# Value products of the one-lane steps on 40 stationary columns in two column halves of the array

## The chip, the core and the metric

The kernel runs on one core of a Trainium2 chip. The metric is device time in microseconds (us) of one execution. PE is TensorE's stream of matmuls and PEld its weight loads, DVE is VectorE, ACT is ScalarE, POOL is GpSimd, and SP is SyncE, whose queue issues nearly all of the DMAs.

## The reference: what is computed

A sequence of 2048 tokens of width 640 passes through two pairs of layers, A B A B, each with a residual and a layer norm ahead of it. A is attention with a recurrent memory: the tokens are cut into 64 segments of 32, and the 8 rows of memory that segment s reads are rows of the output of segment s - 1. So the segments of A are sequential. B is a token mixer and MLP (640 to 640 to 640, 640 to 1536 to 640).

```
for s in range(n_seg):
    h = jnp.concatenate([mem, xs], axis=1)          # 8 + 32 = 40 rows
    q = jnp.einsum('btd,dhe->bhte', h, Wq)          # 32 heads of 192; k and v alike
    scores = jnp.einsum('bhqe,bhke->bhqk', q, k) * scale
    scores = jnp.where(mask[None, None], scores, -1000000000.0)
    p = _softmax(scores, axis=-1)
    o = jnp.einsum('bhqk,bhke->bhqe', p, v)
    o = jnp.einsum('bhte,hed->btd', o, Wo)
    mem = o[:, :M, :].copy()
    outs.append(o[:, M:, :])
```

All is bfloat16 with sums in fp32. The weights of both A layers are the same, and so are those of both B layers.

## The kernel before

**Lanes and steps.** The first A layer is lane 0 and the second is lane 1, five segments behind (LAG, line 22). There are 69 steps. Step t works on segment t of lane 0 and segment t - 5 of lane 1, side by side in one 80-column tile hT (lane 0 in columns 0 to 39, lane 1 in 40 to 79). In steps 0 to 4 only lane 0 has a segment, in steps 64 to 68 only lane 1. These ten are the one-lane steps. In them a product whose moving operand is hT moves 56 columns in place of 80 (ONE, W at line 538).

**Inside a step.** The 32 heads are 8 groups of 4 heads (GW = 768 columns of a weight matrix), taken as 4 pairs of groups. proj_pair (line 549) makes k, q and v of a pair, attend (line 658) does scores, softmax, the product with v and the output product Wo of one group. B is done in chunks of 64 tokens of both lanes, one chunk every two steps, mixed into the steps' work; a last chunk stands alone behind step 68.

**Values.** In a two-lane step v is made transposed, as k and q are: 30 matmuls for each group (line 578), a copy, six transposes (line 616) and two copies into V. In a one-lane step `values` (lines 631 to 658) is called for every pair (V_ONE, line 28). It makes v with tokens as rows: hT is the stationary operand, all 80 columns of it, and the weights move, 384 columns at a time. For each group j of a pair and each half hf of its 768 columns, five matmuls (kc = 0 to 4) add up in one PSUM tile of 80 by 384, so a pair has 20 matmuls in four tiles, each in a bank of its own. Four copies bring them to V: half 0 on ACT (line 656), half 1 on DVE (line 654). The rows of the lane without a segment are computed and copied too. V, like qT, kT, Pm and PT, has one buffer, so V of a group can be written only when the product of the group before has read it.

**Weights.** Of the weight matrices a part stays in SBUF after its first load and the rest is streamed in every step: of the five slices (kc) of a pair, two or three of k, q and v each come through a ring of nine tiles "wst" of 384 KB (RING_A, line 25; issue at line 476), which also wait on SP for a slot to come free. The order of pairs turns round from step to step, so the first pair of a step uses what the last pair of the step before left in the ring (KEEP). B's weights come through a ring of three "wstB" tiles (lines 512 to 518). Wo stays in SBUF after step 0.

**Order.** No loop sets the order of instructions. Each operation is given to a planner (`add`, lines 99 to 138) with its engine, a cost in us, a due time, and what it reads and writes. `place` (from line 140) runs a list schedule with these costs, with PSUM banks and ring slots as resources (class A has six banks, class B two), and the program is written in the order that comes out. An engine runs its instructions in that order. A matmul of n moving columns is put down as max(54, n) / 2400 + 0.0025 us (mm_us), so a group of five value matmuls costs 0.8125 us in the plan.

Of the kernel before, what the change touches and what calls it, by code (L numbers as in the profile page):

```python
# [9 lines left out]
ACT = mybir.ActivationFunctionType  # L10
ALU = mybir.AluOpType
AX = mybir.AxisListType
bf16 = mybir.dt.bfloat16
f32 = mybir.dt.float32
# [7 lines left out]
HG = 4  # L22
# [3 lines left out]
RING_B = 3  # L26
STEP = 48.0
V_ONE = (0, 1, 2, 3)
V_ON = ("ACT", "DVE")
V_PARTS = (range(0, 5),)  # L30
KEEP = True
WO_FROM = 1
AT = (0.0, 0.2, 0.5)
# [9 lines left out]
VT_BUFS = 1  # L43
# [49 lines left out]
class Plan:  # L93
# [8 lines left out]
    def add(self, e, d, due, fn, r=(), w=(), a=(), dma=0, queue=None, margin=0.0, after=()):  # L102
        op = Op()
        op.e, op.d, op.due, op.fn, op.dma, op.margin = e, d, due, fn, dma, margin
        op.succ, op.ready, op.n = [], 0.0, 0
        op.i = len(self.ops)
        op.paced = False
        op.last = None
        op.after = after
        preds = set(after)  # L110
        slots = []
        for b in r:
            preds.update(b.writers)
        for b in w:
            preds.update(b.writers)
            preds.update(b.readers)
        for b in a:
            preds.update(b.base)
            preds.update(b.readers)
        for b in r:  # L120
            b.readers.append(op)
        for b in w:
            b.base = [op]
            b.writers = [op]
            b.readers = []
        for b in a:
            b.writers.append(op)
        for b in {id(b): b for b in (*r, *w, *a)}.values():
            if isinstance(b, Slotted):
                b.left += 1  # L130
                slots.append(b)
        op.slots = slots
        preds.discard(op)
        for p in preds:
            p.succ.append(op)
            op.n += 1
        self.ops.append(op)
        if queue is not None:
            self.queues.setdefault(queue, []).append(op)
        return op  # L140
# [122 lines left out]
def kernel(  # L263
# [16 lines left out]
    nc = tc.nc  # L280
    P = 128
    _, S, Dm = A_x.shape
    H, Dh = A_Wq.shape[1], A_Wq.shape[2]
    M = A_mem0.shape[1]
    SEG = int(A_seg_len)
    NSEG = S // SEG
    F = B_w3.shape[1]
    KC = Dm // P
    FC = F // P
    assert (Dm, F, Dh, H, SEG, M) == (640, 1536, 192, 32, 32, 8) and S % (2 * SEG) == 0 and NSEG > 8  # L290
    NG = H // HG
    GW = HG * Dh
    GC = GW // P
    GWH = GW // 2
    PW = 2 * GW
    NPAIR = NG // 2
    L1 = SEG + M
    NS = 2 * L1
    QD = Dm // 4
    VP = 2 * Dh + 64  # L300
    scale = float(Dh) ** -0.5
# [26 lines left out]
    def ctile(shape, dtype, name):  # L328
        return const.tile(shape, dtype, name=name)
# [35 lines left out]
    Vt = [ctile([NS, 2 * VP], bf16, f"V{i}") for i in range(VT_BUFS)]  # L365
# [3 lines left out]
    Pm = Pmw[:].rearrange("p (c n) -> p c n", c=HG)  # L369
# [42 lines left out]
    def B(*key):  # L412
        key = ALIAS.get(key, key)
        if key not in bufs:
            bufs[key] = Buf()
        return bufs[key]
# [5 lines left out]
    add = plan.add  # L422

    def ps(cls, shape, dtype, name):
        b = Slotted(cls, None)

        def make():
            return psum.tile(shape, dtype, name=name, tag=f"{cls}{b.slot}")
        b.make = make
        return b  # L430

    def T(b):
        if b.obj is None:
            b.obj = b.make()
        return b.obj

    def mm_us(n, m=128, k=1):
        return k * (max(54, n) / 2400.0 + 0.0025)

    def dve_us(n, ps_=True):  # L440
        return ((120 if ps_ else 58) + n) / 960.0 + 0.02

    def act_us(n, ps_=True):
        return ((172 if ps_ else 224) + n) / 1200.0 + 0.02
# [89 lines left out]
    def HX(t):  # L534
        return [B("hT", t % 4, k) for k in ("x0", "m", "xa", "xb", "xc")]

    def attention_step(t):
        ln = lanes(t)
        both = len(ln) == 2
        c0 = 0 if 0 in ln else L1  # L540
        N = NS if both else L1
        NR = c0 + N
# [4 lines left out]
        base = t * STEP  # L547
        sl = STEP / NG
        h = hT[t % 4]
        hk = HX(t)  # L550
# [4 lines left out]
        def proj_pair(i_, pr):  # L555
            s0 = base + sl * 2 * i_
            for kind, at in zip("kqv", AT):
# [9 lines left out]
                for j in range(2):  # L567
# [36 lines left out]
                    else:  # L604
                        V_ = Vt[G % VT_BUFS]

# [12 lines left out]
                        for hf in range(2):  # L619
                            def fe(op, pvt=pvt, V_=V_, hf=hf):  # L620
                                src = T(pvt)[0:NS, GWH * hf:GWH * (hf + 1)].rearrange("n (a b) -> n a b", a=2)
                                v0 = hf * (VP - 64)
                                dst = V_[:, v0:v0 + 512].rearrange("n (a b) -> n a b", a=2)[:, :, 64 * hf:64 * hf + Dh]
                                if hf:
# [5 lines left out]

        def values(i_, pr, s0, wbs, wv):
            nres = KC - STREAM["v"] + MORE.get(("v", pr), 0)
            pv = [[ps("A", [NS, GWH], f32, "psv") for _ in range(2)] for _ in range(2)]
            for j in range(2):
                for hf in range(2):
                    for kcs in V_PARTS:
                        def fv(op, j=j, hf=hf, kcs=kcs):
                            a = GW * j + GWH * hf
                            for kc in kcs:
                                nc.tensor.matmul(out=T(pv[j][hf])[:], lhsT=h[:, kc, :], rhs=wv(kc, a, a + GWH),  # L640
                                                 start=(kc == 0), stop=(kc == KC - 1))
                        rb = [wbs[0]] if kcs[0] < nres else []
                        rb += [wbs[1 + kc - nres] for kc in kcs if kc >= nres]
                        add("PE", mm_us(GWH, k=len(kcs)), s0 + (0.2 * j + 0.05 * hf) * sl, fv,
                            r=(*rb, *hk), a=(pv[j][hf],))
            for j in range(2):
                V_ = Vt[(t * NG + 2 * i_ + j) % VT_BUFS]
                for hf in range(2):
                    def fe(op, j=j, hf=hf, V_=V_):
                        v0 = hf * (VP - 64)  # L650
                        dst = V_[:, v0:v0 + 512].rearrange("n (a b) -> n a b", a=2)[:, :, 64 * hf:64 * hf + Dh]
                        src = T(pv[j][hf])[:].rearrange("n (a b) -> n a b", a=2)
                        if V_ON[hf] == "DVE":
                            nc.vector.tensor_copy(out=dst, in_=src)
                        else:
                            nc.scalar.copy(out=dst, in_=src)
                    add(V_ON[hf], dve_us(GWH) if V_ON[hf] == "DVE" else act_us(GWH), s0 + 0.2 * sl * j, fe, r=(pv[j][hf],),
                        w=(B("V", (t * NG + 2 * i_ + j) % VT_BUFS, hf),))

        def attend(p_, g):  # L660
            G = t * NG + p_
            s0 = base + sl * p_
            q, k_, V_ = qT, kT[G % KT_BUFS], Vt[G % VT_BUFS]
            pss = ps("A", [P, HG * NS], f32, "pss")
            hi = s0 + HI[2] * sl

            def fs(op):
# [8 lines left out]
                r=(B("qT"), B("kT", G % KT_BUFS, 0), B("kT", G % KT_BUFS, 1), B("kT", G % KT_BUFS, 2)), w=(pss,))  # L676
            sm_ = sm[G % 2]
            Pb = Pm
# [8 lines left out]

            def f2(op):
                o = T(pss)[0:NR, 0:HG * N].rearrange("p (a b) -> p a b", a=HG)
                nc.scalar.activation(out=Pb[0:NR, :, c0:c0 + N], in_=o, func=ACT.Exp, bias=sm_[0:NR, 0:1], scale=-1.0)  # L690
            add("ACT", act_us(HG * N) + 0.09, hi - HI[0], f2, r=(pss, smk), w=(Pk,))

            def f3(op):
                nc.vector.tensor_reduce(out=sm_[0:NR, 2:2 + HG], in_=Pb[0:NR, :, c0:c0 + N], axis=AX.X, op=ALU.add)
                nc.vector.reciprocal(out=sm_[0:NR, 6:6 + HG], in_=sm_[0:NR, 2:2 + HG])
                nc.vector.tensor_tensor(out=Pb[0:NR, :, c0:c0 + N], in0=Pb[0:NR, :, c0:c0 + N],
                                        in1=sm_[0:NR, 6:6 + HG].unsqueeze(2).to_broadcast([NR, HG, N]), op=ALU.mult)
            add("DVE", 0.53 + 0.0085 * N, hi - HI[0], f3, w=(Pk, B("sm4", G % 2)))
            pst = ps("A", [P, HG, NS], bf16, "pst")
# [39 lines left out]
            for hf in range(2):  # L739
                def f8(op, hf=hf):  # L740
                    o = T(psy)
                    for cc in range(3 * hf, 3 * hf + 3):
                        for m in range(KC):
                            st = first_wo[0]
                            first_wo[0] = False
                            nc.tensor.matmul(out=o[:, m, cw:cw + W], lhsT=wo[:, cc, m * P:(m + 1) * P],  # L746
                                             rhs=o_[:, cc, 0:W], start=st, stop=True, skip_group_check=True)
                add("PE", mm_us(W, k=3 * KC), due, f8, r=(wb, oks[hf]), a=(psy,))

        for i_ in range(NPAIR):  # L750
            pr = NPAIR - 1 - i_ if t % 2 and KEEP else i_
# [562 lines left out]
    for o in placed:  # L1314
        k = len(nc.cur_bb.bb.instructions)
# [6 lines left out]
        elif o.paced:  # L1322
            k = len(done) - 1
# [39 lines left out]
```

## Time and profile before

| | |
|---|---|
| median of 9 runs | 3435.96 us (3427.66 to 3443.72) |
| the profiled execution | 3437.28 us, span 3435.6 us |
| PE busy | 3329.0 us, 97% of the span |
| PEld busy | 3207.8 us, 93% |
| DVE, ACT, POOL busy | 2394.3 us, 1678.1 us, 236.6 us |
| read from HBM | 817.14 MB, 239 GB/s over the span |
| granted TensorE clock, mean | 0.993 |

Busy time of PE counts a matmul's record from its start to its end, and records of neighbouring matmuls overlap, so its share says little about how much room there is. What a matmul costs in a stream is the distance from its start to the start of the next, called its slot here. A step's borders are taken from the copy at line 765, which runs once near the end of each step and of which the profile has 68, from 89.0 to 3365.2 us.

### The profile page before, as it was taken

The page shows a single profiled execution, that of the slowest core. Times are in us where ns is not written, and L with a number is a line of the kernel's source. Part 1 is how long each engine was busy: PE and PEld are TensorE (multiplying, and loading weights), DVE is VectorE, ACT ScalarE, POOL GpSimd, SP SyncE. Part 2 cuts the span into 40 slices and gives each one's busy share as a digit, 9 for nine tenths or more (in the row PEclk, how much of TensorE's full clock was granted, in tenths as well). Part 3 has the DMA queues.
Part 4 walks back from the last instruction along what each step waited for, and adds up shares of the span by engine and source line. Part 5 has one row for each costly group of instructions (what it writes and reads, how often), then busy time and mean ns, then how long its engine had stood idle before and what let it go on. Part 6 is the DMA issues. An engine that isn't in the chain of part 4 may idle for free.

```text
span 3435.6 us, 183284 instructions
## 1 busy us (share of the span) xinstructions
PE 3329.0 (97%) x82491; PEld 3207.8 (93%) x82493; DVE 2394.3 (70%) x7359; ACT 1678.1 (49%) x4045; POOL 236.6 (7%) x488
## 2 busy tenths in 40 slices
PE   6999999999999999999999999999999999999998
PEld 4889999999999999999999999999999999999886
DVE  2667777777777677777767777776777777767665
ACT  1335555555554555455545555554555555455333
POOL 1000000000000000000000000000000000000000
PEclk8999999999999999999999999999999999999999
DMA  9777667766776686677667766776776677667775
GB/s 373 242 272 261 229 228 250 256 221 223 257 246 224 225 275 233 206 243 256 229 219 265 239 219 232 261 238 220 242 255 224 221 257 247 225 222 273 258 258 188
DMA packets 409739, 834.28 MB, mean 243 GB/s; under 512 B 39632, under 2 KB 207263, under 8 KB 408952
## 3 DMA queue, kind: packets, MB, share of 16 engines
q1 hardware_dynamic: 401656, 809.47, 68.9%
q8 instruction: 645, 10.57, 1.2%
q0 software_dynamic: 7136, 13.00, 1.2%
q14 instruction: 142, 1.16, 0.1%
q10 hardware_dynamic: 160, 0.08, 0.0%
HBM read 817.14 MB, written 5.24 MB: 239 GB/s over the span
## 4 chain that ended last, share of the span: by engine, by line
PE 93%; DMA 3%; issue 2%; ACT 1%; DVE 1%; SPq 1%; POOL 0%; POOLq 0%; ACTq 0%
PE psy L746 16%; PE psq L578 16%; PE psk L578 16%; PE psv L578 15%; PE pvt L616 5%; PE pso L719 4%; PE pss L672 4%; PE psv L640 3%; PE psh L1157 3%; PE y L1202 3%; PE pst L705 2%; PE psh L1035 1%; DMA wst<-in_A_Wv_dram 1%; PE hs L1094 1%; PE psv L808 1%
## 5 line engine op out<-in xcount | busy, mean ns | idle before, releaser
L578 PEld LDWEIGHTS <-wst 128*128 128x128 bf16 x24468 | 993.5, 99 | 23.9 <-issue 11.9
L746 PE MATMUL psy<-oT,wo 128*128 128x80 bf16 (+1 forms) x16560 | 660.2, 200 | 12.2 <-DMA wo<-in_A_Wo_dram 6.8
L746 PEld LDWEIGHTS <-wo 128*128 128x128 bf16 x16560 | 613.3, 99 | 15.1 <-DMA wo<-in_A_Wo_dram 7.6
L588 ACT CAST qT<-psq 128x480 bf16<-128x480 f32 (+1 forms) x552 | 291.7, 528 | 319.5 <-PE psq L578 310.0
L731 DVE CAST oT<-pso 128x240 bf16<-128x240 f32 (+1 forms) x552 | 214.3, 388 | 329.7 <-ACT oT L729 321.4
L578 PE MATMUL psk<-hT,wst 128*128 128x80 bf16 (+1 forms) x9108 | 428.7, 200 | 2.6 <-issue 1.9
L578 PE MATMUL psq<-hT,wst 128*128 128x80 bf16 (+1 forms) x8280 | 399.5, 199 | 4.4 <-issue 2.4
L578 PE MATMUL psq<-hT,wq 128*128 128x80 bf16 (+1 forms) x8280 | 376.9, 200 | 10.7 <-DVE V L625 5.7
L729 ACT CAST oT<-pso 128x240 bf16<-128x240 f32 (+1 forms) x552 | 189.7, 344 | 393.4 <-PE pso L719 369.8
L690 ACT ACTIVATE Pm<-pss,sm 80x320 bf16<-80x320 f32 (+2 forms) x552 | 279.4, 506 | 195.9 <-DVE sm L683 195.1
L578 PE MATMUL psk<-hT,wk 128*128 128x80 bf16 (+1 forms) x7452 | 348.6, 200 | 15.2 <-ACT hT L765 10.8
L578 PE MATMUL psv<-hT,wst 128*128 128x80 bf16 x7080 | 348.3, 202 | 7.4 <-issue 6.1
L602 DVE CAST kT<-psk 64x160 bf16<-64x160 f32 (+1 forms) x1104 | 336.3, 305 | 14.7
L578 PEld LDWEIGHTS <-wq 128*128 128x128 bf16 x8280 | 326.7, 99 | 16.9 <-issue 11.1
L578 PE MATMUL psv<-hT,wv 128*128 128x80 bf16 x7080 | 333.3, 202 | 3.6 <-issue 3.5
L578 PEld LDWEIGHTS <-wk 128*128 128x128 bf16 x7452 | 299.8, 99 | 24.6 <-issue 22.5
L710 ACT COPY PT<-pst 80x320 bf16<-80x320 bf16 (+1 forms) x552 | 222.3, 403 | 202.5 <-PE pst L705 198.5
L683 DVE CUSTOM_DVE_ANT_1 pss<-pss,mask 80x320 f32<-80x320 f32 (+2 forms) x552 | 252.2, 476 | 97.8 <-PE pss L672 94.9
L627 ACT COPY V<-pvt 80x384 bf16<-80x384 bf16 x472 | 223.8, 474 | 191.4 <-PE pvt L616 172.6
L578 PEld LDWEIGHTS <-wv 128*128 128x128 bf16 x7080 | 291.4, 100 | 8.7 <-issue 4.1
L608 ACT CAST vF<-psv 128x480 bf16<-128x480 f32 x472 | 261.8, 555 | 77.1 <-PE psv L578 71.9
L596 DVE CAST kT<-psk 128x320 bf16<-128x320 f32 (+1 forms) x552 | 254.6, 461 | 60.0 <-PE psk L578 53.2
(145 smaller groups left out, 4787.3 us busy)
## 6 DMA issues: line engine op xcount, KB each, us to landing
wst<-in_A_Wk_dram SPq DMA_DIRECT2D x555, 384.0 KB, 5.1
wst<-in_A_Wq_dram SPq DMA_DIRECT2D x486, 384.0 KB, 5.2
wst<-in_A_Wv_dram SPq DMA_DIRECT2D x486, 384.0 KB, 5.3
wstB<-in_B_w_dram SPq DMA_DIRECT2D x495, 320.0 KB, 4.7
wstB<-in_B_w_dram SPq DMA_DIRECT2D x132, 160.0 KB, 4.5
wo<-in_A_Wo_dram SPq DMA_DIRECT2D x8, 960.0 KB, 12.6
xw<-in_A_x_dram POOLq DMA_DIRECT2D x31, 80.0 KB, 5.2
x2d<-vbg POOLq DMA_DIRECT2D x31, 80.0 KB, 5.1
```

What stands on the lines that cost most here:

```text
L578: nc.tensor.matmul(out=o[:, cc, 0:W], lhsT=wv(kc, GW * j + cc * P, GW * j + (cc + 1) * P), rhs=h[:, kc, cw:cw + W], start=(kc == 0 and cc ...
L588: nc.scalar.copy(out=q[:, :, c0:c0 + N], in_=T(pq)[:, :, off:off + N])
L596: nc.vector.tensor_copy(out=k4[:, :, 0::3, c0:c0 + N], in_=p4[:, :, 0::2, off:off + N])
L602: nc.vector.tensor_copy(out=k4[r0:r1, :, jj, c0:c0 + N], in_=p4[r0:r1, :, 1, off:off + N])
L608: nc.scalar.copy(out=vF[:, :, c0:c0 + N], in_=T(pq)[:, :, off:off + N])
L627: nc.scalar.copy(out=dst, in_=src)
L683: nc.vector.tensor_tensor_reduce(out=o, in0=o, in1=maskt.unsqueeze(1).to_broadcast([NR, HG, N]), scale=-scale, scalar=3.0e38, op0=ALU.add, ...
L690: nc.scalar.activation(out=Pb[0:NR, :, c0:c0 + N], in_=o, func=ACT.Exp, bias=sm_[0:NR, 0:1], scale=-1.0)
L710: nc.scalar.copy(out=Pt[:, :, 0:N], in_=T(pst)[0:NS, :, c0:c0 + N])
L729: nc.scalar.copy(out=o_[:, 3:6, off:off + N], in_=T(pso)[:, 3:6, 0:N])
L731: nc.vector.tensor_copy(out=o_[:, 0:3, off:off + N], in_=T(pso)[:, 0:3, 0:N])
L746: nc.tensor.matmul(out=o[:, m, cw:cw + W], lhsT=wo[:, cc, m * P:(m + 1) * P], rhs=o_[:, cc, 0:W], start=st, stop=True, skip_group_check=True)
```

## The change

`values` uses only the 40 columns of hT that belong to the running lane as stationary operand. One PSUM tile of 128 by 384 now holds the same half hf of both groups of a pair: group 0 in partitions 0 to 39, group 1 in partitions 64 to 103. For each half, ten matmuls alternate between the two groups, kc by kc. So a pair still has 20 matmuls of 384 moving columns, now in two operations and two banks. The planner is told 0.8125 + 0.15 us for such an operation of ten matmuls. The four copies to V read 40 partitions and write rows 0 to 39 of V in both lanes, half 0 on DVE and half 1 on ACT.

Since V of lane 1 alone now lies in rows 0 to 39 and no longer in 40 to 79, the softmax tile Pm is written in columns 0 to N for every step, and one memset at step 64 clears its columns 40 to 79. In two-lane steps c0 is 0 and N is 80, so nothing changes there but the order that the planner finds.

```
-V_ON = ("ACT", "DVE")
-V_PARTS = (range(0, 5),)
+V_ON = ("DVE", "ACT")
...
         def values(i_, pr, s0, wbs, wv):
-            pv = [[ps("A", [NS, GWH], f32, "psv") for _ in range(2)] for _ in range(2)]
+            vpart = []
+            for hf in range(2):
+                pv = ps("A", [P, GWH], f32, "psv")
+
+                def fv(op, hf=hf, pv=pv):
+                    o = T(pv)
+                    for kc in range(KC):
+                        for j in range(2):
+                            a = GW * j + GWH * hf
+                            nc.tensor.matmul(out=o[64 * j:64 * j + L1, :], lhsT=h[:, kc, c0:c0 + L1],
+                                             rhs=wv(kc, a, a + GWH), start=(kc == 0), stop=(kc == KC - 1))
+                add("PE", mm_us(GWH, k=KC) + 0.15, s0 + 0.05 * hf * sl, fv, r=(*wbs, *hk), w=(pv,))
+                vpart.append(pv)
             for j in range(2):
                 for hf in range(2):
-                    for kcs in V_PARTS:
-                        def fv(op, j=j, hf=hf, kcs=kcs):
-                            a = GW * j + GWH * hf
-                            for kc in kcs:
-                                nc.tensor.matmul(out=T(pv[j][hf])[:], lhsT=h[:, kc, :], rhs=wv(kc, a, a + GWH),
-                                                 start=(kc == 0), stop=(kc == KC - 1))
...
-                        dst = V_[:, v0:v0 + 512].rearrange("n (a b) -> n a b", a=2)[:, :, 64 * hf:64 * hf + Dh]
-                        src = T(pv[j][hf])[:].rearrange("n (a b) -> n a b", a=2)
+                        dst = Vt[(t * NG + 2 * i_ + j) % VT_BUFS][0:L1, v0:v0 + 512].rearrange("n (a b) -> n a b", a=2)[:, :, 64 * hf:64 * hf + Dh]
+                        src = T(pv)[64 * j:64 * j + L1, :].rearrange("n (a b) -> n a b", a=2)
...
-                nc.scalar.activation(out=Pb[0:NR, :, c0:c0 + N], in_=o, func=ACT.Exp, bias=sm_[0:NR, 0:1], scale=-1.0)
+                nc.scalar.activation(out=Pb[0:NR, :, 0:N], in_=o, func=ACT.Exp, bias=sm_[0:NR, 0:1], scale=-1.0)
...
+        if t == NSEG:
+            def fz(op):
+                nc.vector.memset(Pm[:, :, L1:NS], 0.0)
+            add("DVE", 0.25, base, fz, w=(B("P"),))
```

More of the change, by code (lines that the diff above doesn't have):

```diff
@@ L632, in values, with fe @@
             nres = KC - STREAM["v"] + MORE.get(("v", pr), 0)
-            pv = [[ps("A", [NS, GWH], f32, "psv") for _ in range(2)] for _ in range(2)]
+            vpart = []
[10 more added lines that the diff above has]
+                vpart.append(pv)
             for j in range(2):
                 for hf in range(2):
-                    for kcs in V_PARTS:
-                        def fv(op, j=j, hf=hf, kcs=kcs):
-                            a = GW * j + GWH * hf
-                            for kc in kcs:
-                                nc.tensor.matmul(out=T(pv[j][hf])[:], lhsT=h[:, kc, :], rhs=wv(kc, a, a + GWH),
-                                                 start=(kc == 0), stop=(kc == KC - 1))
[L642 to L649, printed above, removed]
+                    def fe(op, j=j, hf=hf, pv=vpart[hf]):
                         v0 = hf * (VP - 64)
-                        dst = V_[:, v0:v0 + 512].rearrange("n (a b) -> n a b", a=2)[:, :, 64 * hf:64 * hf + Dh]
-                        src = T(pv[j][hf])[:].rearrange("n (a b) -> n a b", a=2)
+                        dst = Vt[(t * NG + 2 * i_ + j) % VT_BUFS][0:L1, v0:v0 + 512].rearrange("n (a b) -> n a b", a=2)[:, :, 64 * hf:64 * hf + Dh]
+                        src = T(pv)[64 * j:64 * j + L1, :].rearrange("n (a b) -> n a b", a=2)
                         if V_ON[hf] == "DVE":
@@ L656, in fe @@
                             nc.scalar.copy(out=dst, in_=src)
-                    add(V_ON[hf], dve_us(GWH) if V_ON[hf] == "DVE" else act_us(GWH), s0 + 0.2 * sl * j, fe, r=(pv[j][hf],),
-                        w=(B("V", (t * NG + 2 * i_ + j) % VT_BUFS, hf),))
+                    add(V_ON[hf], dve_us(GWH) if V_ON[hf] == "DVE" else act_us(GWH), s0 + 0.2 * sl * j, fe,
+                        r=(vpart[hf],), w=(B("V", (t * NG + 2 * i_ + j) % VT_BUFS, hf),))
         def attend(p_, g):
@@ L689, in f2 @@
                 o = T(pss)[0:NR, 0:HG * N].rearrange("p (a b) -> p a b", a=HG)
-                nc.scalar.activation(out=Pb[0:NR, :, c0:c0 + N], in_=o, func=ACT.Exp, bias=sm_[0:NR, 0:1], scale=-1.0)
+                nc.scalar.activation(out=Pb[0:NR, :, 0:N], in_=o, func=ACT.Exp, bias=sm_[0:NR, 0:1], scale=-1.0)
             add("ACT", act_us(HG * N) + 0.09, hi - HI[0], f2, r=(pss, smk), w=(Pk,))
             def f3(op):
-                nc.vector.tensor_reduce(out=sm_[0:NR, 2:2 + HG], in_=Pb[0:NR, :, c0:c0 + N], axis=AX.X, op=ALU.add)
+                nc.vector.tensor_reduce(out=sm_[0:NR, 2:2 + HG], in_=Pb[0:NR, :, 0:N], axis=AX.X, op=ALU.add)
                 nc.vector.reciprocal(out=sm_[0:NR, 6:6 + HG], in_=sm_[0:NR, 2:2 + HG])
-                nc.vector.tensor_tensor(out=Pb[0:NR, :, c0:c0 + N], in0=Pb[0:NR, :, c0:c0 + N],
+                nc.vector.tensor_tensor(out=Pb[0:NR, :, 0:N], in0=Pb[0:NR, :, 0:N],
                                         in1=sm_[0:NR, 6:6 + HG].unsqueeze(2).to_broadcast([NR, HG, N]), op=ALU.mult)
```

## The prediction

> **What bounds the kernel.** I read the page first, then the tables by stretch of the one-lane steps, then the order of time inside one of them, then what PE waits for and how the DMA queues are filled. In the tables the columns are the length, busy us and instructions of PE, PEld, DVE, ACT and POOL, granted clock, DMA share and GB/s.
>
> ```profile
> PE 3329.0 (97%) x82491; PEld 3207.8 (93%) x82493; DVE 2394.3 (70%) x7359; ACT 1678.1 (49%) x4045; POOL 236.6 (7%) x488
> ```
>
> ```profile
> 89.00:260.00 171.00, 164.30 (x4007) 146.08 (x4007) 112.15 (x411) 65.54 (x198) 7.65 (x17) 0.99 0.73 254
> 3188.00:3408.00 220.00, 206.20 (x5028) 181.66 (x5028) 139.61 (x510) 81.23 (x242) 14.04 (x30) 1.00 0.78 271
> 3408.00:3436.00 28.00, 16.42 (x148) 9.86 (x147) 13.50 (x38) 7.52 (x21) 1.66 (x3) 0.98 0.10 34
> 0.00:89.00 89.00, 55.43 (x954) 43.07 (x955) 25.69 (x101) 15.88 (x47) 9.28 (x27) 0.79 1.00 368
> ```
>
> The copy at line 765 puts the end of step 0 at 89, of step 4 at 260, of step 63 at 3188; the last chunk begins near 3408. Step 0 is DMA's: share 1.00 at 368 GB/s, PE busy 62% of it, and its last products wait for Wo (us in all, times, longest).
>
> ```profile
> PE psy L746 <- DMA wo<-in_A_Wo_dram: 6.8, 6, 1.7
> ```
>
> In steps 1 to 4 PE is busy 96%, in steps 64 to 68 94%, DVE about 65%, ACT 38%, DMA 0.73 and 0.78. The slots say it better. If every matmul of a kind is counted with the median distance to the next start, the first stretch has 160 us of slots in 171, the second 203 in 220. So PE sets the length of nine one-lane steps. The value matmuls look like this:
>
> ```profile
> L640 PEld LDWEIGHTS <-hT x800: 113/117/190, 19.4 to 3401.2; 128*80 128x80 bf16 x160
> L640 PE MATMUL psv<-wv,hT x400: 324/326/527, 19.5 to 3400.8; 128*80 128x384 bf16 x134
> ```
>
> ```profile
> 3214.57 0.65 PE L640 MATMUL psv<-wv,hT 128*80 128x384 bf16 x3
> 3215.05 0.49 PE L640 MATMUL psv<-wst,hT 128*80 128x384 bf16 x2
> 3215.38 0.65 PE L640 MATMUL psv<-wv,hT 128*80 128x384 bf16 x3
> 3215.87 0.49 PE L640 MATMUL psv<-wst,hT 128*80 128x384 bf16 x2
> ```
>
> Five matmuls go by from 3214.57 to 3215.38, 0.81 us, 163 ns each; the record of one is 326 ns, twice that, because it also holds the way through the array. A pair has 20: 3.26 us. Nine steps of four pairs have 720: 117.4 us. That is the stock from which the change can take.
>
> **The matmuls.** Their number and their moving columns stay. What may change is the slot. In this trace a slot follows the moving columns: 384 take 163 ns, 80 take 35 whether the stationary operand has 80 or 128 columns (scores, line 672), 56 take 26. So fewer stationary columns alone give nothing. The gain exists only if the two groups, in different column halves, run at once. No row of before has a stationary operand of 64 columns or less beside another, so I bound it: at best two matmuls share a slot (81.5 ns each), 720 x 81.5 = 58.7 us less; at worst they follow one another, 0 less, and if each load then stood outside its slot, 720 x 117 = 84 us more. Loads are no reason against the good end: in the scores the same engine puts 80-column loads and 80-column matmuls at one in 35 ns, and here two loads have 163. I take the good end, for that reason and because the halves share neither outputs nor stationary columns; that the array is fed with two moving operands at once is the part that the trace can't show.
>
> Two statements of the Trainium skill pull apart here. "TensorE: Matmul & The Clock Gate", part 3, says that a load overlaps matmuls in flight only where the row groups differ, and here all matmuls use all rows; the trace has 117 ns loads of the same 128 rows under 163 ns slots, so the row doesn't agree, and by the rule the sum would be the 84 us loss. The same section reports that three column tiles took 2.38 times less than one after another; by that, two halves would give nearly the whole 58.7 us (an estimate), and no run here shows it yet.
>
> **Going in and out of halves.** The array must be emptied where it passes from whole to halved use, if the two can't overlap. Bounds: nothing, and one tail of a record plus one load, 326 - 163 + 117 = 280 ns. I take the tail, 163 ns, the nearest row. How often: the 720 matmuls now stand in 78 uninterrupted runs in PE's order, 2.17 for each pair of four operations, so 1.17 of its 3 inner borders are broken. With two operations there is one border, broken 0.39 times: 36 x 1.39 = 50 runs, 100 passages, 16.3 us (0 to 28; with all borders broken, 144 passages and the high price, 40). "TensorEngine Tiling (Array Packing)", Key Properties, has the rule that a change of tiling mode drains TensorE; no row here shows such a change, and by the rule the price is not zero.
>
> So 58.7 - 16.3 = 42.4 us, 4.7 for a step, 1.18 for a pair.
>
> **What is late next.** DVE at 65% of 43 us has 28 us of work for a step of 38, ACT 16. DMA is tighter. In step 65 (3231 to 3277):
>
> ```profile
> DMA  0197999999999999999899999999995000000000
> GB/s 0 40 260 200 361 361 354 364 364 402 399 392 406 362 377 353 384 300 359 251 357 346 340 414 393 397 387 381 399 403 203 23 14 0 0 0 0 14 0 0
> ```
>
> These are 40 slices of 3231 to 3278. DMA is full for some 33 us and then rests, as the ring holds what the next step's first pair needs. In the full part it can't go faster. I set each transfer's landing beside the first matmul that reads it: the median lead of the streamed slices in one-lane steps is 3.0 to 3.6 us (k, q) for a step's second pair, 5.4 to 6.2 for the third, 3.7 to 5.9 for the fourth; the shortest are about 2. PE would reach the fourth pair 3 x 1.18 = 3.5 us sooner. Step 65: its last q slice landed 2.3 us ahead of use, 1.2 too late then; step 66: its last v slice 2.5 us ahead, 1.0 too late. One us a step, 9 us, is given back (0 to 20: at worst about half of the saving, when the shortest leads decide). 42.4 - 9 = 33 us.
>
> **Step 0** keeps its length, as its DMA does. If PE counted there too, it would be four pairs more, 6.5 us of gain; for the range.
>
> **Copies.** 80 on DVE (554 ns) and 80 on ACT (474 ns) as before, same columns, 40 partitions in place of 80; I take the same durations. They only change places: half 0, which PE makes first, goes to DVE, the busier engine. DVE's third of idle time covers it; if not, V of a group is later by at most the 80 ns difference, 72 x 0.08 = 6 us at worst. V of group 0 can start after the first half of both groups, 0.81 + 0.16 us after its first matmul, before at 0.81 us. Where lane 1 runs alone the softmax works on columns 0 to 39, same sizes. The memset is one 0.2 us DVE instruction by this row:
>
> ```profile
> L402 DVE MEMSET Pm<- 80x160 uint32 x1 | 0.2, 192 | 0.0
> ```
>
> **Banks and waits.** The bank of a pair is freed only when both groups are copied, and group 1's copy waits until group 0's product has read V. That held two of six banks before, and does after; in between, two fewer are taken. PE's idle time ahead of line 640 outside step 0 is 1.6 us, so at most that is gained. No wait is added on DMAs: every group already waited for all slices of its pair.
>
> **Order.** The planner sees 1.925 us for 3.25 a pair, so it writes a new order for all steps. Two-lane steps keep costs, dues and resources; I put them at 0. A chance order costs little: single two-lane steps reach 54.2 us beside usual 47.5 to 51. Two such more or fewer are 7 us either way.
>
> **Sum.** 3437.28 (the profiled execution: span 3435.6 and 1.7 around it) - 33 = 3404 us. The median shown is 1.3 us lower, which I leave out. Own range of this case: 3437 - 58.7 is 3378, and with 40 us of passages and 9 given back 3428.
>
> **Rivals.**
> (1) The halves run one after the other, and the passages are paid: 3437 + 16 = 3454 us, up to 3538 if the loads show too. For it: all rows of before are of one stream through the array. Against it: a slot holds moving columns alone, and outputs, loads and stationary columns of the halves are apart. It decides from the mean distance between value matmuls: above 163 - 16.3 / 720 = 140 ns the change loses.
> (2) The halves overlap, but DMA gives nearly all back: three streamed pairs of a step need their 33 us, and the last v slice is followed by the last pair's attention (in step 65 its landing is 35 us behind the step's start, and 11 us remain). If PE stands in front of every pair, and passages cost 280 ns (28 us), 58.7 - 28 - 20 leaves 10; with a worse order of the two-lane steps, 3430 to 3443. For it: DMA full in the stream phase. Against it: leads of 3 to 6 us.
> (3) The edit is no change in kind: the program emits whole-array matmuls for the 40 columns. Then slots stay at 163 without passages, 3437 us, and the records would still show 720 slots of 163. The start partitions 0 and 64 speak against it.
>
> **Numbers.** The forecast case 0.70, (1) 0.20, (2) 0.07, (3) 0.03. A measurement of this kernel tells about 0.2% from no change, 7 us. So faster 0.70, same 0.10, slower 0.20. The range, 3376 to 3446, takes in the forecast's case, (2), (3) and step 0's share at the low end; it leaves out most of (1).
>
> **What would show it.** Right: value matmuls start in couples, ten in 0.8 to 0.9 us, with a gap of 0.1 to 0.3 us at both ends of a run; steps 1 to 4 and 64 to 68 are 3 to 5 us shorter each, step 0 and the 59 two-lane steps are not; DMA share in the one-lane stretches rises to some 0.85, with a few PE waits for wst. Wrong: ten matmuls in 1.6 us; or short runs of them and long idle time for wst behind them; or a change of the two-lane steps above 7 us in sum.

## The result, and the profile after

The changed kernel takes 3422.89 us (median of 10 runs, 3414.16 to 3427.11), before 3434.33 us (32 runs); the ratio is 0.9962, interval 0.9952 to 0.9972. So it is faster, by 11 to 13 us, and not by the 33 us of the forecast. The profiled execution took 3427.11 us, the longest of the ten, with a span of 3425.3, 10.3 less than that of before.

The two lines of the page on the engines and on the DMA queue that fetches instructions:

```profile
PE 3292.3 (96%) x82491; PEld 3161.0 (92%) x82493; DVE 2396.3 (70%) x7360; ACT 1679.4 (49%) x4045; POOL 237.2 (7%) x488
...
q8 instruction: 645, 10.57, 1.2%
```

The number of PE's instructions is the same, and its busy time fell by 37 us, of which the span shows 10. The second line (packets, MB, share) is used below.

The one-lane stretches, steps 1 to 4 and steps 64 to 68, as a table by stretch:

```profile
89.00:257.00 168.00, 150.35 (x4015) 127.93 (x4015) 112.68 (x411) 65.54 (x199) 7.92 (x17) 0.98 0.74 259
3186.00:3397.00 211.00, 187.77 (x5024) 157.64 (x5024) 140.51 (x508) 82.56 (x242) 14.26 (x30) 0.99 0.79 278
```

They were 171 and 220 us long, and are 168 and 211. That is 1.3 us for each of the nine steps, where the forecast named 3 to 5 as its sign. PE was busy 96% and 94% of them, now 89% and 89%. DMA share and GB/s hardly rose. Step 0 ends at 89.0 us in both, and steps 5 to 63 take 2928.8 us in place of 2927.4.

The value matmuls in the order of time:

```profile
3222.30 0.51 PE L641 MATMUL psv<-wv,hT 128*40 128x384 bf16 x4
3222.64 0.65 PE L641 MATMUL psv<-wst,hT 128*40 128x384 bf16 x6
3223.23 0.37 PE L717 MATMUL pso<-PT,V 80*128 80x40 bf16 x8
3223.53 0.51 PE L641 MATMUL psv<-wv,hT 128*40 128x384 bf16 x4
3223.86 0.66 PE L641 MATMUL psv<-wst,hT 128*40 128x384 bf16 x6
```

Ten matmuls go by in 0.81 us, where five did before. The couples start 2 to 5 ns apart, and the next couple 163 ns later. So the halves overlap fully, and the loads (min/median/max in ns) lie under the slots:

```profile
L641 PEld LDWEIGHTS <-hT x800: 94/100/158, 19.4 to 3390.3; 128*40 128x40 bf16 x160
```

A run that follows other work starts 84 to 99 ns later than the slot of the matmul ahead of it says (median 92), and what follows a run starts 98 ns late: 190 ns for each run. Before, both were 0 to 3 ns. Such a delay at the entry or the exit of a run is called a passage below.

### A ledger of PE's time

To see where the gain went I added up, in the two stretches, the distance from each matmul's start to the next. A matmul gets the median distance of its kind as its slot; what is over is a wait, put down to what ended it. "Block" is a wait at a fixed place in PE's stream, explained below it. The rows of the experiments are used later. All in us, each from one profiled execution.

| kernel | sum | values | passages | other slots | block | ACT, DVE | weights | other |
|---|---|---|---|---|---|---|---|---|
| before | 390.9 | 117.5 | 0 | 245.9 | 18.8 | 5.9 | 0.6 | 1.9 |
| after | 379.1 | 60.0 | 12.0 | 245.6 | 29.8 | 20.3 | 5.8 | 4.3 |
| nostream | 341.7 | 59.7 | 13.2 | 247.8 | 1.3 | 17.8 | 0 | 1.3 |
| nostream_before | 368.6 | 117.5 | 0 | 247.4 | 0 | 3.5 | 0 | 0.2 |
| nostream_nonorm | 328.7 | 59.6 | 12.2 | 247.5 | 2.8 | 4.1 | 0 | 1.5 |
| wide | 359.5 | 59.6 | 12.0 | 242.7 | 9.0 | 20.8 | 12.4 | 1.2 |
| wide_before | 381.0 | 117.5 | 0 | 242.5 | 8.3 | 6.6 | 1.7 | 3.3 |
| split | 390.9 | 67.6 | 7.0 | 247.1 | 39.8 | 19.8 | 3.5 | 4.5 |
| turn | 384.6 | 72.1 | 12.0 | 247.4 | 23.4 | 19.7 | 4.8 | 4.0 |
| one_run | 396.2 | 59.5 | 6.8 | 247.3 | 28.5 | 33.5 | 7.5 | 11.5 |
| plan_serial | 375.8 | 60.6 | 13.0 | 246.4 | 20.0 | 17.7 | 10.5 | 6.0 |
| rate350 | 387.4 | 60.0 | 12.8 | 247.7 | 16.0 | 33.6 | 5.9 | 9.8 |
| copies_back | 393.8 | 59.6 | 11.3 | 248.2 | 28.5 | 29.1 | 7.6 | 7.9 |
| before_copies | 396.2 | 117.5 | 0 | 246.8 | 20.6 | 5.8 | 3.3 | 1.7 |

(In "split" the last matmul of a run is counted too long and its passage too short; their sum, 74.6, is right. A row's parts miss its sum by up to 2 us of distances that differ from their median by less than 15 ns.)

Values and passages together fell by 45.5 us. The waits rose by 33: 11 at block borders, 14 for ACT and DVE, 5 for weights, 2 others.

How far a row can be trusted (the runs named here are explained below): `turn`, `split` and `wide` run every engine's operations in the order of the changed kernel, as their cost in the plan is the same, and their two-lane steps have the same program. Yet these steps took 2920.9, 2915.2 and 2923.6 us in their profiled executions against 2928.8. So a few us between two rows show nothing by themselves. That the waits rose by 20 us or more is safe: in the four kernels that reorder the same work (`one_run`, `plan_serial`, `rate350`, `copies_back`) they sum to 54 to 81 us, against 27 and 31 in `before` and `before_copies`. The split into 11, 14, 5 and 2 is that of one execution of one order.

"Other" goes with the time at half clock. The profile shows a granted clock of 0.5 in windows of 3.41 us, or two of them in a row. Behind the first 5 us of the first stretch, which in every kernel begin at 0.5, the stretches of `before`, `nostream` and `wide` have no such window ("other" 1.9, 1.3 and 1.2 us). The changed kernel has two, from 106.6 and from 3243.5 us, in or just behind two of its longest waits (at 104.96 and 3239.47 us); `copies_back` has five, `rate350` and `one_run` eight each (7.9, 9.8 and 11.5 us).

**What a block border is.** This is PE in the order of time, at one long wait:

```profile
3217.73 0.47 PE L577 MATMUL psq<-hT,wq 128*128 128x56 bf16 x12
3218.04 0.55 PE L577 MATMUL psq<-hT,wst 128*128 128x56 bf16 x15
3220.82 0.25 PE L577 MATMUL psq<-hT,wst 128*128 128x56 bf16 x3 [2.23 <-issue]
3220.91 0.26 PE L744 MATMUL psy<-oT,wo 128*128 128x56 bf16 x4
```

The wait stands inside one group of six matmuls that all read tiles which are there, and the profile names no releaser ("issue"). If all rows of PE (matmuls, loads and its 87 semaphore and drain instructions) are numbered in order, then in the changed kernel 27 of the 28 gaps over 1 us between 89 and 3390 us come at the same place modulo 256, and in the kernel before 23 of 24. The instruction queue has 645 packets of 16 KB, and 645 x 256 is 165,120, PE's 165,071 rows and a rest. After each such gap over 0.4 us PE starts again 1.2 to 1.9 us (median 1.43) after one of these packets has landed. In the example the packet ran from 3218.41 to 3219.35, PE stopped at 3218.40 and went on at 3220.82. PE had run out of fetched instructions.

### The profile page after: what moved, and what is told of

It reads as the page before. It is cut to its first block, busy times and chain, and to the rows that moved or that the text cites. A ratio compares the mean times of both kernels' runs of the same rounds, so it can differ in the third digit from the quotient of the medians.

```text
span 3425.3 us, 183229 instructions
## 1 busy us (share of the span) xinstructions
PE 3292.3 (96%) x82491; PEld 3161.0 (92%) x82493; DVE 2396.3 (70%) x7360; ACT 1679.4 (49%) x4045; POOL 237.2 (7%) x488
## 4 chain that ended last, share of the span: by engine, by line
PE 91%; DMA 4%; issue 2%; DVE 2%; ACT 1%; SPq 1%; POOL 0%; POOLq 0%; ACTq 0%; DVEq 0%
PE psy L744 16%; PE psq L577 16%; PE psk L577 16%; PE psv L577 15%; PE pvt L615 5%; PE pso L717 4%; PE pss L670 4%; PE psh L1160 3%; PE y L1205 3%; PE pst L703 2%; PE psv L641 1%; PE psh L1038 1%; PE hs L1097 1%; DMA wst<-in_A_Wv_dram 1%; DMA wst<-in_A_Wq_dram 1%
## 5 line engine op out<-in xcount | busy, mean ns | idle before, releaser
L727 ACT CAST oT<-pso 128x240 bf16<-128x240 f32 (+1 forms) x552 | 189.7, 344 | 366.2 <-PE pso L717 341.7
```

The lines of the kernel that those rows point to most:

```text
L727: nc.scalar.copy(out=o_[:, 3:6, off:off + N], in_=T(pso)[:, 3:6, 0:N])
```

## The experiments

All ratios are to the kernel before, run on the same chip. Distances in us between two kernels are those of their medians; from chip to chip the median of the kernel before was 3431.3 to 3434.3 us, so they can be off by some 3 us more than the intervals say.

**Streamed weights left out.** `nostream` and `nostream_before` take the transfers out of the nine steps.

```
+            pr0 = pr
...
-                if i_ == 0 and t > 0 and KEEP:
-                    wbs, wv = kept[kind]
+                pr = pr0
+                if t > 0 and (i_ == 0 or not both):
+                    wbs, wv, pr = kept[kind]
...
-                    kept[kind] = wbs, wv
+                    kept[kind] = wbs, wv, pr
```

> The changed kernel, in whose one-lane steps behind step 0 all four pairs use the k, q and v weights of the step's first pair, which lie in SBUF already: some 24 transfers of 384 KB fewer in each of nine steps, the same instructions on PE, DVE and ACT; it computes with the wrong weights there. Theory W (the streamed weights, and the contention on the DMA engines with them, take the gain back): 25 to 35 us faster than the changed kernel, and PE's long waits go. Theory F (PE runs out of fetched instructions whatever the DMA engines do): the waits at every 256th instruction stay, under 10 us faster. Theory C (the chain of scores, softmax and copies sets the length): under 10 us faster, with the waits for DVE and ACT as they are.

> The kernel before with the same cut of the streamed weights in its one-lane steps. It says what the change is worth when DMA is nearly idle there. Theory W: the kernel before gains little by the cut (its PE waited 10 us in steps 1 to 4 and 17 in steps 64 to 68, most of it for instructions), 5 to 20 us, and the distance between the two kernels grows from 11 us to 30 to 45. Theories F and C: the distance stays at 10 to 20 us.

Measured: 0.9839 (0.9818 to 0.986; 3377.45 us) and 0.9927 (0.991 to 0.9944; 3409.33 us). The two first lines are of nostream, the other two of nostream_before:

```profile
88.50:239.30 150.80, 146.61 (x4034) 126.09 (x4034) 111.81 (x411) 67.12 (x198) 7.90 (x17) 0.99 0.20 59
3153.80:3345.80 192.00, 183.28 (x5046) 156.47 (x5043) 139.37 (x510) 82.03 (x243) 14.56 (x30) 1.00 0.29 89
```

```profile
88.70:251.30 162.60, 161.84 (x4015) 144.79 (x4015) 111.50 (x411) 66.26 (x199) 7.64 (x17) 0.99 0.18 54
3174.90:3381.30 206.40, 204.60 (x5030) 181.12 (x5030) 139.91 (x513) 81.67 (x243) 14.28 (x31) 1.00 0.27 83
```

With DMA at 59 and 89 GB/s the same work of PE runs 37 us shorter in the stretches (45 by the medians, more than the 25 to 35 expected; the plan is made anew, and in the profiled execution the two-lane steps were 14 us shorter too). The distance of the two kernels grows from 11 to 32 us by the medians, 27 in the ledger. Theory W holds in the main for the size. But what went is above all the wait at block borders, 29.8 to 1.3 us; waits for the weights themselves were only 5.8. So the fetch is late only with the weights' traffic beside it: theory F, "whatever the DMA engines do", is wrong, and so is W where it means late weights. It starts late rather than being slow. In these stretches a packet takes 1.04 us in the changed kernel and 0.97 in nostream (medians), but half of the fetches start with under 147 rows of PE left to the border where it stops, four with under 20; in nostream the median is 222 and the least 129. What holds the start back isn't in the profile. Theory C holds for what is left: 17.8 us for ACT and DVE stay, against 3.5 in the kernel before.

**Fewer instructions, and more.** `wide` and `wide_before` give PE the same time with 160 matmuls fewer a step, `split` gives it 80 more. All three keep the order of operations of the kernel that they start from.

```
+                    if not both:
+                        for m in range(KC):
...
+                            nc.tensor.matmul(out=o[:, m0:m0 + 3, cw:cw + W], lhsT=wo[:, 3 * hf, m * P:(m + 1) * P],
+                                             rhs=o_[:, 3 * hf:3 * hf + 3, 0:W], start=st, stop=True, skip_group_check=True)
+                        return
```

```
+                    for q0 in range(0, GWH, GWH // 2):
+                        for kc in range(KC):
+                            for j in range(2):
...
+                                nc.tensor.matmul(out=o[64 * j:64 * j + L1, q0:q0 + GWH // 2], lhsT=h[:, kc, c0:c0 + L1],
+                                                 rhs=wv(kc, a, a + GWH // 2), start=(kc == 0), stop=(kc == KC - 1))
```

> The changed kernel, whose output products in one-lane steps take 10 matmuls of 168 columns in place of 30 of 56 for each group: the same time of PE (0.73 us against 0.78) with 40 instructions fewer of some 240, the same DMA; the output product is wrong there. Theory F (PE runs out of fetched instructions): the long gaps at the borders of fetched blocks, 30 us in the one-lane stretches of the changed kernel, fall to 15 us or less, and the total by 10 to 18 us. Theory W and theory C: only the slots count, 3 to 5 us less.

> The kernel before with 10 output products of 168 columns in place of 30 of 56 for each group in one-lane steps (the output product is wrong there). Its waits at block borders in these steps were 19 us, against 30 after the change; with fewer instructions both should nearly go. Theory: 12 to 20 us faster than the kernel before, and the distance to the changed kernel with the same edit (22 us faster than without) grows from 11 us to 15 to 22. If fetch had no part in the lost gain, the distance stays at 11.

> The changed kernel with every value matmul of 384 columns cut into two of 192, all slices of the first part ahead of the second: 36 pairs x 20 more matmuls, each with its load, 1440 more instructions of PE behind step 0 (8% more in these steps), the same moving columns, and 720 x 2.5 ns / 2 = 1 us more of slots where the halves overlap. If fetched instructions are what PE waits for: 5 to 6 more blocks of 256, the waits at block borders in the one-lane steps rise from 30 us to 33 to 40, and the total by 3 to 10 us. If they are not: within 2 us of the changed kernel.

(`split` adds 720 matmuls and 720 loads; the sum of 1440 is the one that was meant. `wide` takes 20 matmuls and 20 loads out of each group, eight groups a step.)

Measured: wide 0.9907 (0.9886 to 0.9927; 3400.93 us), wide_before 0.9973 (0.9964 to 0.9982; 3422.01), split 1.0007 (0.9997 to 1.0017; 3433.21). The stretches of wide:

```profile
89.00:248.30 159.30, 146.71 (x3374) 124.25 (x3373) 112.75 (x411) 65.33 (x198) 7.93 (x17) 0.99 0.76 272
3171.90:3372.60 200.70, 185.68 (x4230) 154.28 (x4228) 141.58 (x513) 82.59 (x243) 14.27 (x30) 1.00 0.82 292
```

A sixth of the matmuls fewer, at a higher DMA rate than before the edit, and the stretches are 20 us shorter, of which slots are 3. The block waits fell from 29.8 to 9.0 us, and waits for weights rose from 5.8 to 12.4: where PE no longer runs dry, the weights step in. In wide_before block waits fell by 10.5, and the distance of the two kernels grew from 11 to 21 us. The sizes were not those expected: `wide` gained 22 us in place of 10 to 18, `wide_before` 9 in place of 12 to 20. In split block waits rose by 10, and the total by 10 us by the medians, nearly the whole of what the change had gained (its profiled execution was the shortest of its twelve, that of the changed kernel the longest of its ten, so those two spans hide it). PE's largest waits in the second stretch of split (us in all, times, longest), all without a releaser:

```profile
PE psq L577 <- issue: 10.2, 8, 1.9
PE psy L745 <- issue: 4.7, 4, 2.0
PE psv L642 <- issue: 2.6, 2, 1.6
PE psk L577 <- issue: 2.0, 2, 1.5
PE psn L812 <- issue: 1.3, 1, 1.3
```

So the rate at which PE uses instructions up costs time by itself. It came with the change: the value matmuls of a pair were 20 in 3.26 us, against 38 a us in k and q, and are now 20 in 1.63. That the fetch caught up in the time of the slow ones is likely, but no run shows it by itself.

**A shorter chain.** `nostream_nonorm` also leaves out the sums, the inverse and the multiplication of the softmax.

```
-            add("DVE", 0.53 + 0.0085 * N, hi - HI[0], f3, w=(Pk, B("sm4", G % 2)))
+            if both:
+                add("DVE", 0.53 + 0.0085 * N, hi - HI[0], f3, w=(Pk, B("sm4", G % 2)))
```

> The changed kernel without streamed weights in its one-lane steps (as in nostream, 3377 us), and there also without the three DVE instructions that sum the softmax rows, invert and multiply (the weights and the scaling are wrong there): about 0.9 us of DVE less in the chain from scores to values for each group. In nostream PE still waited 17 us for ACT and DVE in these steps, 3.5 in the kernel before with the same cut. If it is the length of this chain, with one buffer for each of its tiles, those waits fall by half or more and the total by 7 to 14 us. If it is the order of the plan, or other waits step in, under 4 us.

Measured: 0.9819 (0.9806 to 0.9831), 3368.76 us, 8.7 less than nostream (13 less in the stretches). The waits for ACT and DVE fell from 17.8 to 4.1 us, as expected of the chain. First nostream, then nostream_nonorm, PE's waits of over half a us in the second stretch:

```profile
PE psy L746 <- ACT oT L729: 2.4, 6, 0.5
PE psy L746 <- DVE oT L731: 1.6, 3, 0.7
PE pso L719 <- ACT PT L710: 1.3, 2, 0.6
PE psy L746 <- issue: 1.0, 2, 0.6
PE psk L579 <- ACT hT L770: 0.8, 3, 0.3
PE psq L579 <- ACT PT L710: 0.8, 2, 0.4
```

```profile
PE psy L747 <- issue: 2.0, 3, 0.9
PE psk L579 <- ACT hT L771: 0.8, 3, 0.3
PE psx L929 <- DVE yTB L779: 0.5, 1, 0.5
```

PE waited for the copies that end a group's chain (oT, PT), though neither engine was full (DVE 73% over the two stretches). Of the changed kernel's variants only this one has PE's slots set the length again: values, passages and other slots are 319 of 329 us.

**The order of the two groups, one run, the plan, the rate.**

```
-                    for kc in range(KC):
-                        for j in range(2):
+                    for j in range(2):
+                        for kc in range(KC):
```

> The changed kernel with the two loops over slices and groups exchanged: in each half the five matmuls of group 0 come first, then the five of group 1, with the same 40 columns, halves of the array, bank and cost in the plan. Only the last of group 0 and the first of group 1 can share a slot, so a half takes about 9 x 163 = 1.47 us in place of 0.81, 72 times: 47 us more of PE's slots. Theory 1 (PE is no longer what sets the length of the one-lane steps; of the 46 us of slots that the change freed, some 34 came back as waits of PE): the total rises by far less than 47 us, 10 to 20 us, to about the time of before, as the waits go back. Rival (PE's slots still set the end, and the 46 us were lost elsewhere): 40 to 47 us more.

Measured: 0.9967 (0.9953 to 0.998), 3422.44 us, the same as the change. As a test of PE's slots it is weak, since its premise failed. In the order of time:

```profile
3216.59 0.52 PE L641 MATMUL psv<-wv,hT 128*40 128x384 bf16 x3
3216.93 0.33 PE L641 MATMUL psv<-wst,hT 128*40 128x384 bf16 x1
3216.95 0.33 PE L641 MATMUL psv<-wv,hT 128*40 128x384 bf16 x1
3217.09 0.67 PE L641 MATMUL psv<-wst,hT 128*40 128x384 bf16 x5
```

The program has two matmuls on wv and three on wst for group 0, then the same for group 1. The chip started the third wv, which is group 1's first, with the second of group 0, and its fourth ahead of group 0's last two. So it doesn't keep the program's order between the halves, and the halves overlap anyhow, one slot of 0.18 us late. That was 12 us more of value time, not 47. The ledger has 5.5 us of it, as the block waits were 6.4 us less with the slower stream in the same order; the medians show nothing.

> The changed kernel with both halves of a pair in one operation of 20 matmuls, so 36 runs of them in PE's order behind step 0 in place of 64, and 28 passages in and 28 out fewer at 92 and 98 ns: 5.3 us of PE's time less. If PE's time were what counts, 5 us faster than the changed kernel (0.9947 of before in place of 0.9962). By the theory that PE now waits for fetched instructions, weights and the chain of softmax and copies, under 2 us, or slower by up to 5 since V's first half is ready later.

```
+            vpart = [ps("A", [P, GWH], f32, "psv") for _ in range(2)]
+
+            def fv(op):
+                for hf in range(2):
...
+            add("PE", mm_us(GWH, k=2 * KC) + 0.15, s0, fv, r=(*wbs, *hk), w=tuple(vpart))
```

Measured: 1.0014 (1.0003 to 1.0026), 3436.11 us, 13 us slower than the change, although the passages fell from 12.0 to 6.8 us. Waits for ACT and DVE rose by 13 us, and others by 7, with eight windows at half clock in place of two. The sign was expected, the size was not.

> The changed kernel, whose planner is told 1.625 us for a half of the values, what it would cost one after the other, in place of 0.9625; the program differs only in the order of its operations. If the order that follows from the plan's cost holds the gain back (PE's waits for the chain, 15 us more than before), the total moves by 5 us or more; if the waits come from DMA and instruction fetch, it stays within 4 us of the changed kernel.

```
-                add("PE", mm_us(GWH, k=KC) + 0.15, s0 + 0.05 * hf * sl, fv, r=(*wbs, *hk), w=(pv,))
+                add("PE", mm_us(GWH, k=2 * KC), s0 + 0.05 * hf * sl, fv, r=(*wbs, *hk), w=(pv,))
```

Measured: 0.9976 (0.9964 to 0.9987), 3423.56 us, within 1 us of the change by the medians (the intervals of the two ratios overlap). So it isn't the cost that the planner is told that holds the gain back.

> The changed kernel, whose planner reckons with 350 KB per us for the DMAs of one-lane steps in place of 400, so that it holds weight transfers back further (the profile shows 340 to 390 when full). If fetched instructions are late because they stand behind weight transfers that were issued early, fewer of these stand in the queues, the waits at block borders (30 us in the one-lane steps) fall by 5 us or more, and the total by 3 to 8. If the fetch is late merely because PE is fast, no difference of more than 3 us.

```
-RATE_ONE = 400.0e3
+RATE_ONE = 350.0e3
```

Measured: 0.9985 (0.9975 to 0.9995), 3425.53 us. Half of the expectation came true: block waits fell from 29.8 to 16.0 us. But in the new order waits for ACT and DVE rose by 13, and the total doesn't gain. That it was the shorter queue which made the fetch faster, and not the new order, isn't told apart by this run.

**The engines of the copies.**

> The changed kernel with the copies of V on the engines of before, half 0 on ACT and half 1 on DVE. In the changed kernel PE waits 3.9 us for ACT's copy to V in one-lane steps and none for DVE's. If that is the exchange, 2 to 5 us faster; if the wait is for V as such, or belongs to the order of the plan, within 3 us either way.

> The kernel before with the copies of V exchanged as the change has them, half 0 on DVE and half 1 on ACT, and nothing else. The changed kernel without this exchange was no faster than before (ratio 1.000), so it could be that the exchange is the gain by itself. If so, 8 to 14 us faster than before. By the theory that PE's slots set the length of the one-lane steps before the change, where it waited only 6 us for ACT and DVE, the exchange alone is worth under 4 us, and it matters only once PE has been made shorter.

```
-V_ON = ("DVE", "ACT")
+V_ON = ("ACT", "DVE")
```

(The diff is that of copies_back; before_copies is its reverse on the kernel before.) Measured: copies_back 1.0000 (0.9987 to 1.0012), 3431.44 us; before_copies 1.0025 (1.0012 to 1.0038), 3440.26 us. Neither expectation held. Without the exchange the change gains nothing: values and passages are as short as with it, and the waits are 13 us longer, 9 of them for ACT and DVE. The exchange alone makes the kernel before slower by 8 us, so it isn't the gain by itself. Whether it is the engines or the order of all operations, which the planner makes anew, these two runs don't say.

## Why the prediction was wrong

**Right: the matmuls.** The good end was taken, and 720 matmuls went from 117.5 us to 60.0, 57.5 less against 58.7. The rule on loads that the forecast set against it (the Trainium skill, "TensorE: Matmul & The Clock Gate", part 3) had no effect: the loads, 100 ns each, lie under the slots though all rows are shared. The 2.38 for three tiles, quoted beside it, is 79% of a full overlap, which taken alone is less than the "nearly the whole" read from it; measured is 98%.

**Right in size: the passages.** 16.3 us were forecast, 12.0 measured, as 64 runs of 190 ns in place of 50 of 326: more runs, and neither a whole tail going in nor one coming out. The Trainium skill ("TensorEngine Tiling (Array Packing)", Key Properties) states a drain at a change of tiling mode; the delays seen here, 92 and 98 ns, agree with it.

**Right: step 0, the two-lane steps, the engines' own work.** 89.0 us in both, 1.4 us more, and DVE and ACT busy as before.

**Wrong: the step "One us a step, 9 us, is given back".** Of the 45.5 us, 33 were given back. The step looked only at weight slices, and for these it was near: 5 us. Two waits are missing from it, put at nothing (another 2 us of "other" came with the half clock).

The first is instruction fetch, 11 us. It could have been seen: in the second stretch of before the six largest of PE's waits (us in all, times, longest) were put down to "issue", 11 us in sum, and I passed over these rows because they name no releaser.

```profile
PE psy L746 <- issue: 3.6, 2, 1.9
PE pss L672 <- issue: 2.4, 2, 1.6
PE psv L640 <- issue: 1.6, 1, 1.6
PE psq L578 <- issue: 1.4, 1, 1.4
PE hs L1094 <- issue: 1.1, 1, 1.1
PE pso L719 <- issue: 1.1, 1, 1.1
```

After the change the six largest there are again "issue", 17 us in sum. Waits at block borders were already 18.8 us, twice what the forecast gave back.

The second is the chain behind "DVE at 65% of 43 us has 28 us of work for a step of 38, ACT 16", 14 us. That counts work and not the length of a chain: copies, scores, softmax, transposes and products of a group follow one another through single buffers, and PE has less of other work to lay between. nostream_nonorm shows that the length of the chain is what PE waits for when DMA is out of the way: its plan too is a new one, but no other order of the changed kernel went under 17.7 us for ACT and DVE.

**Too small: "a chance order costs little", 7 us.** Edits that leave the work alone, or nearly, and make a new plan (one_run, plan_serial, rate350, copies_back) put the changed kernel anywhere from 3424 to 3436 us, and before_copies is 8 us above before. An order is worth as much as this change gained, so part of the 11 to 13 us, and of the 33 given back, may be luck of the order.

**The rivals.** (1) and (3) are out: the slots halved. (2) named DMA, and DMA had a part in 16 of the 33 us, 5 directly and 11 through the instruction fetch that comes late beside it; the rest is the chain and the half clock. Its price, 10 us left of the gain, is near the measured one, but by another working: the passages were cheaper than it said and PE did not stand before every pair's weights. The share of DMA rose to 0.74 and 0.79, not to 0.85.

**What stays open.** What lets a fetch begin isn't in the profile: some start with 160 or more of the fetched instructions left, some only when PE has stopped, as at 3218.41. And how much of the 14 us for ACT and DVE is the chain as such and how much this plan's order can't be split while DMA is full; the kernel with streamed weights and a shorter chain was not run.

## What to carry to other kernels

When an engine that is 95% busy is made shorter, write down every kind of wait that it already has, those without a releaser too, and ask of each whether it grows as the engine speeds up. Count instructions as well as time: here a stream of short matmuls was limited by the fetch of its instructions while weights were streamed, 29.8 us of 379, and hardly without them, 1.3 of 342. Where a planner rewrites the order, two or three edits that change only the order tell how large a difference can be and still be chance, and one profiled execution doesn't.

## What the runs showed that was not expected

- PE's instructions come in packets of 16 KB, 256 at a time (645 packets for 165,071 rows). In the kernel before 42 waits of over 0.4 us at their borders take 45.5 us of the whole span; after a landing PE needs another 1.2 us or more.
- Those waits nearly vanish in the one-lane steps when the weights aren't streamed (29.8 to 1.3 us), though a packet's own time is about 1.0 us in both; it is the start of the fetch that comes later.
- Matmuls of the two column halves start out of the program's order. The Trainium skill, "TensorE: Matmul & The Clock Gate", part 3, says that matmuls start and end strictly in order; in turn the second group's first matmul began with the first group's second.
- Two column halves with different moving operands of 128 rows run at the full rate each, 384 columns in 163 ns; changing between whole array and halves costs 92 ns going in and 98 ns coming out.
